# Block products in four groups, plain halves first, two fronts ahead, and raw x added when it is loaded for the fold

## The chip, the cores and the metric

The kernel runs on one core of a Trainium2 chip. The metric is the device time in microseconds (us) of one execution; lower is better. A profiled execution also has a span, from its first instruction to its last, and a granted TensorE clock (1.00 is full speed). TensorE is PE in the profile, VectorE DVE, ScalarE ACT, GpSimd POOL, and SP is the engine whose queue issues the transfers here.

## The reference

The input x has 2048 tokens of 448 channels. Cut to what is computed:

```
xn = layernorm(x)
A  = irfft2(rfft2(xn) * (w_r + i w_i))                  # spectral filter
h  = gelu(layernorm(xn) @ w1), four channel quarters shifted by +1, -1, +2, -2 tokens
x1 = xn + shifted(h) @ w2
B  = x1 + gelu(layernorm(x1) @ w3) @ w4                 # w3: 448 -> 1792, w4: 1792 -> 448
out = x + A + B
```

## The kernel before, in words

Each float32 operand of a large product is split into two float16 halves, and a product is three matmuls: high by high, high by low, low by high. The 2048 tokens are 16 blocks `b` (tokens a*16 + b); `xt` holds the running state of each block, read with `xb(b)`, in a scale that the factor `p12` undoes. The work runs in five stages: the first layer norm with w1 and w2 (to about 87 us); the MLP of group 0 (to about 112 us); the fold and first half of the transform beside the MLP of groups 1 and 2 (to about 190 us); the filter, 16 chunks, beside groups 2 to 4 (to about 275 us); the inverse transform, one block after another, beside groups 4 to 7.

**The MLP.** A group `G` (0 to 7) is two blocks, 256 tokens, and it is done in seven units `fp`, each of 256 of the 1792 hidden columns. `front(G, fp)` (L755) makes 22 matmuls of 256 columns into a PSUM bank `pw` (L433), applies the gelu on ACT (L763), and splits the result into the halves `hf`: high on ACT (L767), low on DVE (L768). `back(G, fp)` (L778) multiplies by w4. A plain unit makes 12 matmuls of 448 columns into `acc` (L798). A unit for which `crossed(G, fp)` holds (groups in `STR`) keeps only the 4 high-by-high matmuls of 448 columns. Its other two passes are block products with seven small products instead of eight (a Strassen form): three more DVE instructions make the combined operands `hg` (L771 to L773), 14 matmuls of 224 columns go to `acc` and to a second pair of banks `cr` (L809), and at the group's end ACT copies the banks `cr` to `cross` (L826) and POOL joins them (L829, L833; DVE does this for group 7). The combined weights come from `w4_forms` on POOL, once, for all groups. At a group's end `evacuate` (L815) adds `acc`, times a factor `k34`, to the state (L818).

`mlp(Gs, ahead)` (L837) sets the order in the program: `back` of a unit comes after the fronts of the next `ahead` units. Groups 0 to 2 have `ahead=AH=2`; later calls have 1. A scheduler then orders the instructions of each engine by priority, with `behind(...)` as a pin behind another instruction; matmuls of the MLP fill what the other stages leave. `hf` has three buffers, `hg` two, `pw` two banks.

**The fold.** `do_fold(b0)` (L568) loads raw x of two blocks into `xf` (three buffers; L571), normalizes it in place on ACT (L575), folds it on POOL (L580 to L583); `step1_in` splits it (ACT L591, DVE L592), `step1` multiplies (PE L601) and stores (ACT L605, DVE L606).

**The inverse.** `inv_a(b)` (PE `pe` L724, ACT L728, POOL L731 and L732, DVE L733 to L736, ACT L738, DVE L739) and `inv_b(b)` (PE `py` L746), which adds the filter's result to the state (DVE L747). For blocks 0 to 11 `finish(b)` (L560) then loads raw x into one of two row buffers `xr` (L556), adds `p12` times the state to it (DVE L557) and stores it (L561). Blocks 12 to 15, whose group is done last, have their raw x added into buffers in `x2mem` by the same L557 before the last `evacuate`.

Of the kernel before, what the change touches and what calls it, by code (L numbers as in the profile page):

```python
# [16 lines left out]
ALU = mybir.AluOpType  # L17
# [14 lines left out]
AH = 2  # L32
# [3 lines left out]
WMAX = [(1, 4), (1, 5), (2, 0), (2, 0), (2, 1), (2, 2), (2, 3), (2, 4)]  # L36
LATE = [(2, 2), (2, 3), (2, 4), (2, 5)]
HS = 3
STR = (5, 6, 7)
INV, LAG = 4, 2  # L40
EVAC, FILL = 0, 100000

# [80 lines left out]
def body(tc, nc, x, wf, w1, w2, w3, w4, c_g, c_n, c_small, out):  # L123
# [429 lines left out]
    def unscaled(b, t=None):  # L553
        if t is None:
            t = row()[:, :D]
        SY.dma_start(t, xv[:, b])  # L556
        V.scalar_tensor_tensor(out=t, in0=xb(b), scalar=p12, in1=t, op0=ALU.mult, op1=ALU.add)  # L557
        return t

    def finish(b):  # L560
        SY.dma_start(ov[:, b], unscaled(b))  # L561


    OFF = [0, 113, 225, 338, 450]
    FAM = [0, 2, 1, 3]
    folds = {}

    def do_fold(b0):  # L568
        f = pfd.tile([128, 2, 4, 113], F32, tag="xf", bufs=3, name=f"xf{b0}")
        X = f.rearrange("p b s d -> p (b s d)")[:, 0:2 * D + 2].rearrange("p (b d) -> p b d", b=2)  # L570
        after["X", b0] = (SY.dma_start(X[:, :, 0:D], xv[:, b0:b0 + 2]).ins,)  # L571
        with behind("f", *FOLD[b0 // 2]):
            for i in range(2):
                x_ = X[:, i, 0:D]
                A.activation(out=x_, in_=x_, func=AF.Identity, scale=xn_scale[b0 + i], bias=xn_bias[b0 + i])  # L575
            A.activation(out=X[:, :, D:D + 1], in_=X[:, :, 0:1], func=AF.Copy)
        ad = X[:, :, 0:D].rearrange("p b (h d) -> p h b d", h=2)[:, :, :, 0:113]
        bc = X[:, :, 1:D + 1].rearrange("p b (h d) -> p h b d", h=2)[:, ::-1, :, 223:110:-1]
        u = xr.rearrange("p (a b s d) -> p a b s d", a=2, b=2, s=2)
        P.tensor_tensor(out=u[:, 0], in0=ad, in1=bc, op=ALU.add)  # L580
        P.tensor_tensor(out=u[:, 1], in0=ad, in1=bc, op=ALU.subtract)
        for k, op in ((0, ALU.add), (2, ALU.subtract)):
            i = P.tensor_tensor(out=f[:, :, k:k + 2].rearrange("p b s d -> p s b d"), in0=u[:, :, 0], in1=u[:, :, 1], op=op)  # L583
        after["fold", b0] = (i.ins,)
        for i in range(2):
            folds[b0 + i] = f[:, i].rearrange("p s d -> p (s d)")
# [33 lines left out]
    def w_scale_end(wm):  # L620
        t = pc.tile([128, 4], F32, name="wt")
        V.tensor_reduce(out=t[:, 0:1], in_=wm, axis=AX.X, op=ALU.max)
        pt = bank("sp", "wpt")
        T.transpose(pt[0:1, 0:128], t[:, 0:1], ident)
        V.tensor_reduce(out=t[0:1, 1:2], in_=pt[0:1, 0:128], axis=AX.X, op=ALU.max)
        V.tensor_scalar(out=t[0:1, 1:2], in0=t[0:1, 1:2], scalar1=2.0 ** -20, scalar2=None, op0=ALU.max)
        pb = bank("sp", "wpb")
        T.matmul(pb[:, 0:1], ones[0:1], t[0:1, 1:2], start=True, stop=True)
        e = pc.tile([128, 3], I32, name="we")
        V.tensor_copy(out=t[:, 2:3], in_=pb[:, 0:1])  # L630
        V.tensor_single_scalar(e[:, 0:1], t.bitcast(I32)[:, 2:3], 0x7F800000, op=ALU.bitwise_and)
        V.tensor_single_scalar(e[:, 1:2], e[:, 0:1], 0x7F800000, op=ALU.bitwise_xor)
        V.tensor_scalar(out=sc[:, 0:1], in0=e.bitcast(F32)[:, 1:2], scalar1=ZPRE, scalar2=None, op0=ALU.mult)
        for h in range(2):
            V.tensor_scalar(out=sc[64 * h:64 * h + 64, 2:3], in0=sc[64 * h:64 * h + 64, 0:1], scalar1=2.0 * h - 1.0,
                            scalar2=None, op0=ALU.mult)
        V.tensor_scalar(out=sc[:, 1:2], in0=e.bitcast(F32)[:, 0:1], scalar1=2.0 ** -21 / (ZPRE * UPRE * VPRE),
                        scalar2=s12[:, 0:1], op0=ALU.mult, op1=ALU.mult)


    stream, pfs, zs = {}, {}, {}
# [100 lines left out]
    def inv_b(b):  # L742
        vh = vhs.pop(b)
        py = bank("sp", f"py{b}")
        for n, (vi, ri) in enumerate(PASS):
            T.matmul(py[:, :D], cV[ri], vh[:, vi], start=n == 0, stop=n == 2)  # L746
        V.scalar_tensor_tensor(out=xb(b), in0=py[:, :D], scalar=sc[:, 1:2], in1=xb(b), op0=ALU.mult, op1=ALU.add)  # L747


    acc, xs, hs, hg, rest = {}, {}, {}, {}, {}  # L750
# [27 lines left out]
    def back(G, fp):  # L778
        h = hs.pop((G, fp))
        n = D // 2  # L780
        end = 4 if G == 7 else 6
        if fp == 0:
            acc[G] = [bank("acc", f"acc{G}{i}") for i in range(2)]
            if G in STR:
                xs[G] = [bank("tr", f"cr{G}{i}") for i in range(2)]
        if (G, fp) == (7, 5):
            xs[G] = [bank("tr", f"end{i}") for i in range(2)]
        C = [[(slice(0, D), acc[G][i][:, 0:D], 0, 6)] for i in range(2)]
        if G == 7:
            C[1] = [(slice(0, D), acc[G][1][:, 0:D], 0, 4)]  # L790
            if fp > 4:
                C[1] = [(slice(n * k, n * k + n), xs[G][k][:, 0:n], 5, 6) for k in range(2)]
        for i in range(2):
            for r, to, s, e in C[i]:
                with behind("m", G, fp) if (G, fp) == (7, 6) and ("m", G, fp) in after else contextlib.nullcontext():
                    for f in range(2):
                        for hi, wi in ((0, 0),) if crossed(G, fp) else ((0, 0), (0, 1), (1, 0)):
                            m = T.matmul(to, h[:, hi, 2 * f + i], w4p[0][:, wi, 2 * fp + f, r],  # L798
                                         start=fp == s and f == 0 and hi + wi == 0, stop=fp == e and f == 1 and hi == 1)
                after["m", G, fp] = (m.ins,)  # L800
        if crossed(G, fp):
            g = hg.pop((G, fp))
            X = [xs[G][k // 2][:, n * (k % 2):n * (k % 2) + n] for k in range(4)]
            H = [[acc[G][i][:, n * k:n * k + n] for k in range(2)] for i in range(2)]
            forms = [(0, 1, X[0], 9), (1, 3, H[1][0], 9), (3, 2, H[0][0], C[0][0][3]), (6, 4, X[2], 9),
                     (4, 5, X[3], end), (5, 6, X[1], end), (2, 7, H[1][1], C[1][0][3])]
            for hi, wi in ((0, 1), (1, 0)):
                for k, slot, to, e in forms:
                    m = T.matmul(to, h[:, hi, slot] if slot < 4 else g[:, hi, slot - 4], w4f[fp][k][wi], start=k in (0, 6) and fp == 0 and hi == 0,  # L809
                                 stop=hi == 1 and fp == e)  # L810
            after["m", G, fp] = (m.ins,)
        k34 = p34[:, 1:2] if G >= 6 else p34[:, 0:1]
        to = {i: rest[2 * G + i] if G >= 6 else xb(2 * G + i) for i in range(2)} if fp >= 4 else {}

        def evacuate(i):  # L815
            for r, src, _, e in C[i]:
                if fp == e:
                    V.scalar_tensor_tensor(out=to[i][:, r], in0=src, scalar=k34, in1=to[i][:, r], op0=ALU.mult, op1=ALU.add)  # L818
                    if G == 7 and fp == 6:
                        SY.dma_start(ov[:, 2 * G + i, r], to[i][:, r])  # L820

        with prio(EVAC):
            if G in STR and fp == end:
                e0, e1 = cross[:, 0], cross[:, 1]
                for i in range(2):
                    A.activation(out=cross[:, i], in_=xs[G][i][:, 0:D], func=AF.Copy, scale=k34)  # L826
                for o, x, y in ((e0[:, n:], e0[:, 0:n], e0[:, n:]), (e1[:, 0:n], e1[:, 0:n], e0[:, n:]),
                                (e0[:, n:], e0[:, n:], e1[:, n:]), (e1[:, n:], e1[:, 0:n], e1[:, n:])):
                    (V if G == 7 else P).tensor_tensor(out=o, in0=x, in1=y, op=ALU.add)  # L829
            for i in range(2):  # L830
                evacuate(i)
                if G in STR and fp == end:
                    (V if G == 7 else P).tensor_tensor(out=to[i], in0=to[i], in1=cross[:, 1 - i], op=ALU.add)  # L833
                if G == 6 and fp == 6:
                    SY.dma_start(ov[:, 2 * G + i], to[i])
# [235 lines left out]
    xh_buf = [pfd.tile([128, 2 * 452 + 16], F16, name=f"xh{i}") for i in range(4)]  # L1071
    for i in range(4):
        P.memset(xh_buf[i][:, 904:], 0.0)
    mlp([1, 2], ahead=AH, tags=("mm", "tr"))
    for b in range(0, NB, 2):
        do_fold(b)
        step1_in(b)
        step1_in(b + 1)
        with behind("m", *PACE[b // 2]):
            step1(b)  # L1080
            step1(b + 1)
# [24 lines left out]
        if 0 <= i - 3 < NC:  # L1106
            chunk_c(i - 3)
    close("pst")
    mlp(range(3, 6))
    pv = pool("pv", side="right")  # L1110
    bs = [*range(12, 16), *range(8, 12), *range(8)]
    units = [(G, fp) for G in range(4, 8) for fp in range(7)][INV:]
# [11 lines left out]
                    finish(bs[n - 1])  # L1124

    inverse(range(4))
    mlp([6], last=True)
    inverse(range(4, 17))
    mlp([7], last=True)
    for name in ("pv", "pa2", "pa", "pw", "px", "pc", "ps"):  # L1130
# [25 lines left out]
```

## Time and profile before

| | |
|---|---|
| median of 3 runs | 410.98 us (409.61 to 411.87) |
| the profiled execution: time, span | 411.11 us, 409.2 us |
| granted clock | 1.00 |
| PE busy | 402.4 us, 98% of the span |
| DVE busy | 313.3 us, 77% |
| ACT busy | 268.2 us, 66% |
| POOL busy | 164.1 us, 40% |
| moved by DMA | 49.46 MB, mean 121 GB/s |

The busy time of PE is no measure of how well it is fed, since matmuls are pipelined: a record of 448 columns lasts 352 ns in the page's groups, though the next one starts 189 ns later (12 in 2.27 us in the chain). A wait of PE is therefore read from the starts: the time from one start to the next, less the step at which such matmuls follow each other undisturbed.

### The profile page before, as it was taken

The page shows a single profiled execution, that of the slowest core. Times are in us where ns is not written, and L with a number is a line of the kernel's source. Part 1 is how long each engine was busy: PE and PEld are TensorE (multiplying, and loading weights), DVE is VectorE, ACT ScalarE, POOL GpSimd, SP SyncE. Part 2 cuts the span into 40 slices and gives each one's busy share as a digit, 9 for nine tenths or more (in the row PEclk, how much of TensorE's full clock was granted, in tenths as well). Part 3 has the DMA queues.
Part 4 walks back from the last instruction along what each step waited for, and adds up shares of the span by engine and source line. Part 5 has one row for each costly group of instructions (what it writes and reads, how often), then busy time and mean ns, then how long its engine had stood idle before and what let it go on. Part 6 is the DMA issues. An engine that isn't in the chain of part 4 may idle for free.

```text
span 409.2 us, 8827 instructions
## 1 busy us (share of the span) xinstructions
PE 402.4 (98%) x3379; PEld 295.4 (72%) x3379; DVE 313.3 (77%) x674; ACT 268.2 (66%) x465; POOL 164.1 (40%) x260
## 2 busy tenths in 40 slices
PE   8999999999999999999999999999999999999996
PEld 3554555666677877677878887877788888878885
DVE  5989998898654737975899988841698969898645
ACT  4699993984838766754788888757566555644332
POOL 3889820002297745599321212100133234434300
PEclk9999999999999999999999999999999999999999
DMA  8999999907710356527367567320000202332201
GB/s 280 352 264 181 170 178 259 270 2 156 159 48 0 94 207 198 158 24 179 94 173 157 144 149 181 98 60 2 1 2 2 69 22 77 107 108 76 88 2 45
DMA packets 57209, 49.46 MB, mean 121 GB/s; under 512 B 41312, under 2 KB 52192, under 8 KB 57168
## 3 DMA queue, kind: packets, MB, share of 16 engines
q1 hardware_dynamic: 57168, 48.91, 46.3%
q8 instruction: 26, 0.43, 0.4%
q14 instruction: 15, 0.12, 0.1%
HBM read 35.06 MB, written 3.67 MB: 95 GB/s over the span
## 4 chain that ended last, share of the span: by engine, by line
PE 68%; DVE 12%; ACT 7%; DMA 6%; issue 3%; POOL 1%; SPq 0%; ACTq 0%; DVEq 0%; POOLq 0%
PE pw L433 23%; PE acc L798 18%; PE pw L462 6%; PE pw L507 6%; PE cr L809 3%; DMA wl<-wf 2%; PE acc L809 2%; ACT te L680 2%; PE ps L601 2%; PE py L746 2%; PE pe L724 2%; DVE te L683 1%; DVE te L681 1%; PE pu L704 1%; DMA h<-hs 1%
## 5 line engine op out<-in xcount | busy, mean ns | idle before, releaser
L433 PE MATMUL pw<-x2mem,w3p 128*128 128x256 f16 x1232 | 151.4, 272 | 0.0
L433 PEld LDWEIGHTS <-w3p 128*128 128x128 f16 x1232 | 118.8, 98 | 18.4
L798 PE MATMUL acc<-w4p,hf 128*128 128x448 f16 x508 | 106.7, 352 | 0.2 <-DVE xt L818 0.2
L798 PEld LDWEIGHTS <-hf 128*128 128x128 f16 x532 | 51.6, 98 | 37.1 <-issue 0.4
L768 DVE SCALAR_TENSOR_TENSOR hf<-pw,h,hf 128x512 f16<-128x512 f32 x56 | 41.8, 747 | 35.3 <-ACT hf L767 35.0
L763 ACT ACTIVATE pw<-pw,pe 128x512 f32<-128x512 f32 x56 | 36.7, 655 | 42.5 <-PE pw L433 42.4
L731 POOL TENSOR_TENSOR e<-e 128x226 f32<-128x226 f32 x16 | 12.8, 801 | 72.0 <-ACT e L728 67.9
L767 ACT ACTIVATE hf<-pw,h 128x512 f16<-128x512 f32 x56 | 38.3, 685 | 1.3
L507 PE MATMUL pw<-w2p,h 112*128 112x448 f16 x192 | 38.9, 352 | 0.1
L685 POOL TENSOR_TENSOR xr<-te 128x450 f32<-128x450 f32 x16 | 16.2, 1012 | 56.5 <-DVE te L683 50.6
L462 PE MATMUL pw<-w1p,w4x 128*128 128x448 f16 x176 | 34.9, 352 | 0.5 <-DVE h L936 0.5
L507 PEld LDWEIGHTS <-h 112*128 112x128 f16 x192 | 18.5, 98 | 16.8 <-DMA h<-x2mem 0.8
L462 PEld LDWEIGHTS <-w4x 128*128 128x128 f16 x176 | 17.0, 98 | 16.5 <-ACT w4x L422 0.7
L728 ACT ACTIVATE e<-pe 128x452 f32<-128x452 f32 x16 | 8.7, 544 | 20.7 <-PE pe L724 20.7
L580 POOL TENSOR_TENSOR xr<-xf 128x452 f32<-128x452 f32 x8 | 8.9, 1109 | 27.0 <-issue 16.0
L716 ACT ACTIVATE U<-y 113x512 f16<-113x512 f16 x32 | 18.0, 619 | 0.0
L592 DVE TENSOR_TENSOR xh<-xf,xh 128x452 f16<-128x452 f32 x16 | 14.0, 907 | 5.0 <-ACT xh L591 5.0
L680 ACT ACTIVATE te<-px 64x450 f32<-64x450 f32 x32 | 17.3, 539 | 0.6
L583 POOL TENSOR_TENSOR xf<-xr 128x452 f32<-128x452 f32 x16 | 16.7, 1066 | 0.6
L809 PE MATMUL cr<-w4x,hg 128*128 128x224 f16 x102 | 15.8, 259 | 0.1
L809 PEld LDWEIGHTS <-hg 128*128 128x128 f16 x152 | 14.7, 98 | 1.2 <-DVE hg L772 0.5
L738 ACT ACTIVATE vh<-e 128x448 f16<-128x448 f32 x16 | 9.2, 573 | 8.8 <-DVE e L736 8.8
(201 smaller groups left out, 773.1 us busy)
## 6 DMA issues: line engine op xcount, KB each, us to landing
wc<-wf SPq DMA_DIRECT2D x32, 225.0 KB, 3.7
wl<-wf SPq DMA_DIRECT2D x8, 450.0 KB, 3.7
xf<-x SPq DMA_DIRECT2D x8, 448.0 KB, 3.6
xt<-x SPq DMA_DIRECT2D x3, 896.0 KB, 11.0
w3raw<-w SPq DMA_DIRECT2D x3, 896.0 KB, 14.4
xr<-x SPq DMA_DIRECT2D x12, 224.0 KB, 2.6
out<-xr SPq DMA_DIRECT2D x12, 224.0 KB, 2.0
gn<-c_g SPq DMA_DIRECT2D x16, 128.0 KB, 3.3
```

The costliest lines, as they stand in the source:

```text
L433: T.matmul(ps_out, wp[:, wi + t, cols], xT[:, xi + t, tok], start=t == 0 and wi + xi == 0, stop=t == 3 and wi == 4)
L462: m = T.matmul(pm[:, :D], xTs[g][:, xi + t, 128 * i:128 * i + 128], w1p[:, wi + t], start=t == 0 and p == 0, stop=t == 3 and p == 2)
L507: m = T.matmul(w2b[b][:, :D], hT[g][:112, 4 * hi + k, o:o + 128], w2p[:, wi, k], start=k == 2 and hi + wi == 0, stop=k == 3 and hi == 1)
L583: i = P.tensor_tensor(out=f[:, :, k:k + 2].rearrange("p b s d -> p s b d"), in0=u[:, :, 0], in1=u[:, :, 1], op=op)
L680: i = A.activation(out=e[64 * h:64 * h + 64], in_=px_[64 - 64 * h:128 - 64 * h, :2 * DF], func=AF.Copy)
L685: P.tensor_tensor(out=z, in0=t[:, 0], in1=t[:, 1], op=ALU.add)
L716: A.activation(out=U[b][:113, p].rearrange("p q (c k) -> p q c k", c=NC), in_=Y1[:113, p, :, :, b], func=AF.Copy)
L763: A.activation(out=pm, in_=pm, func=AF.Gelu_apprx_tanh, scale=r3)
L767: i = A.activation(out=h[:, 0], in_=pv_, func=AF.Copy, scale=h3)
L768: j = V.scalar_tensor_tensor(out=h[:, 1], in0=pv_, scalar=h3, in1=h[:, 0], op0=ALU.mult, op1=ALU.subtract)
L798: m = T.matmul(to, h[:, hi, 2 * f + i], w4p[0][:, wi, 2 * fp + f, r], start=fp == s and f == 0 and hi + wi == 0, stop=fp == e and f == 1 a ...
L809: m = T.matmul(to, h[:, hi, slot] if slot < 4 else g[:, hi, slot - 4], w4f[fp][k][wi], start=k in (0, 6) and fp == 0 and hi == 0, stop=hi ...
```

## The change

Group 4 is computed by block products too. In the crossed units, all matmuls whose left operand is a plain half come before those with a combined operand. Groups 3 to 6 run with two fronts ahead. For the block pairs in `EARLY` (blocks 2 to 11) raw x is added to the state, times `p12`, when x has been loaded for the fold; `inv_b` then uses a factor that contains `p12`, the evacuations use the unscaled factor, and `finish` stores straight from the state. The first three fold loads are written ahead of the MLP of groups 1 and 2.

```diff
+EARLY = (2, 4, 6, 8, 10)
-STR = (5, 6, 7)
+STR = (4, 5, 6, 7)
...
     def finish(b):
-        SY.dma_start(ov[:, b], unscaled(b))
+        SY.dma_start(ov[:, b], xb(b) if b // 2 * 2 in EARLY else unscaled(b))
...
-    def do_fold(b0):
+    Xs = {}
+
+    def load_fold(b0, pin):
         f = pfd.tile([128, 2, 4, 113], F32, tag="xf", bufs=3, name=f"xf{b0}")
         X = f.rearrange("p b s d -> p (b s d)")[:, 0:2 * D + 2].rearrange("p (b d) -> p b d", b=2)
         after["X", b0] = (SY.dma_start(X[:, :, 0:D], xv[:, b0:b0 + 2]).ins,)
+        Xs[b0] = f, X
+        if b0 in EARLY:
+            with behind("f", *pin):
+                for i in range(2):
+                    V.scalar_tensor_tensor(out=xb(b0 + i), in0=xb(b0 + i), scalar=p12, in1=X[:, i, 0:D], op0=ALU.mult, op1=ALU.add)
+
+    def do_fold(b0):
+        f, X = Xs.pop(b0)
         with behind("f", *FOLD[b0 // 2]):
...
+        V.tensor_tensor(out=sc[:, 3:4], in0=sc[:, 1:2], in1=p12, op=ALU.mult)
...
-        V.scalar_tensor_tensor(out=xb(b), in0=py[:, :D], scalar=sc[:, 1:2], in1=xb(b), op0=ALU.mult, op1=ALU.add)
+        V.scalar_tensor_tensor(out=xb(b), in0=py[:, :D], scalar=sc[:, 3:4] if b // 2 * 2 in EARLY else sc[:, 1:2], in1=xb(b),
+                               op0=ALU.mult, op1=ALU.add)
...
-            for hi, wi in ((0, 1), (1, 0)):
-                for k, slot, to, e in forms:
+            for hi, wi, part in ((0, 1, 0), (1, 0, 0), (0, 1, 1), (1, 0, 1)):
+                for k, slot, to, e in forms[3 * part:3 + 4 * part]:
...
-        k34 = p34[:, 1:2] if G >= 6 else p34[:, 0:1]
+        k34 = p34[:, 1:2] if G else p34[:, 0:1]
...
+    for b in (0, 2, 4):
+        load_fold(b, (0, 6))
     mlp([1, 2], ahead=AH, tags=("mm", "tr"))
     for b in range(0, NB, 2):
+        if b > 4:
+            load_fold(b, FOLD[b // 2])
         do_fold(b)
...
-    mlp(range(3, 6))
+    mlp(range(3, 6), ahead=AH)
...
-    mlp([6], last=True)
+    mlp([6], last=True, ahead=AH)
```

## The prediction

> **What bounds the kernel now.** I read the page first, then the chain of waits in order of time, then the busy times by stage.
>
> ```profile
> PE 402.4 (98%) x3379; PEld 295.4 (72%) x3379; DVE 313.3 (77%) x674; ACT 268.2 (66%) x465; POOL 164.1 (40%) x260
> ```
>
> PE is busy throughout by its records, but records overlap the next matmul, so the share says neither how well PE is fed nor what a removed matmul is worth. The chain shows both. Its columns are start, length, what.
>
> ```profile
> 104.14 2.40 PE pw L433 x22
> 106.54 2.27 PE acc L798 x12
> 108.81 2.40 PE pw L433 x22
> ...
> 344.16 1.95 DMA out<-xr
> 346.12 2.92 DMA xr<-x
> ...
> 385.47 2.40 PE pw L433 x22
> 387.88 0.76 PE acc L798 x4
> 389.97 2.40 PE pw L433 x22
> ```
>
> A front follows a back without a gap in nearly all of the run: PE is the bound, by the work that it is given, and each matmul costs its step (2.40/22 = 0.109 us for 256 columns, 2.27/12 = 0.189 for 448). A plain unit takes 108.81 - 104.14 = 4.67 us, a crossed one 389.97 - 385.47 = 4.50, of which the 14 small matmuls are 389.97 - 387.88 - 0.76 = 1.33 (0.095 each). Only around 335 to 362 us does the chain leave PE for DVE and for the row buffer that is stored and loaded again (1.95 and 2.92 us at 344 to 349). Busy times by stage (length, then PE, PEld, DVE, ACT, POOL, then clock, DMA share and GB/s):
>
> ```profile
> 112.50:145.00 32.50, 32.50 (x281) 24.18 (x279) 17.78 (x23) 20.82 (x39) 27.69 (x30) 1.00 0.20 58
> ...
> 190.00:250.00 60.00, 59.54 (x629) 48.10 (x626) 52.28 (x92) 48.18 (x88) 18.00 (x21) 1.00 0.64 158
> 250.00:270.00 20.00, 20.00 (x197) 15.93 (x195) 15.23 (x25) 14.05 (x25) 3.92 (x4) 1.00 0.39 102
> 270.00:285.00 15.00, 15.00 (x128) 11.00 (x126) 4.77 (x7) 9.92 (x19) 0.00 (x0) 1.00 0.09 26
> 285.00:330.00 45.00, 45.00 (x426) 36.69 (x424) 35.38 (x82) 26.71 (x48) 11.57 (x16) 1.00 0.07 22
> 330.00:362.00 32.00, 31.73 (x302) 26.02 (x300) 27.17 (x61) 17.63 (x32) 13.62 (x18) 1.00 0.23 73
> 362.00:385.00 23.00, 23.00 (x210) 19.08 (x209) 20.58 (x43) 10.45 (x17) 10.03 (x12) 1.00 0.30 101
> ```
>
> DVE is the second engine: 52.3 of 60 us in the filter, 83.1 of 100 us in the inverse stage (285 to 385). What PE loses to it is read from the starts, in the timeline of PE:
>
> ```profile
> 242.73 0.42 PE L658 MATMUL pp<-csm,y 113*128 113x112 f16 x5
> 243.42 0.74 PE L675 MATMUL px<-x2mem,gn 128*128 128x225 f16 x6 [0.28 <-DVE te L681]
> ...
> 341.91 0.82 PE L433 MATMUL pw<-x2mem,w3p 128*128 128x256 f16 x6
> 342.93 0.73 PE L746 MATMUL py<-vh,csm 128*128 128x448 f16 x3 [0.20 <-DVE xt L747]
> ...
> 357.83 0.60 PE L433 MATMUL pw<-x2mem,w3p 128*128 128x256 f16 x4
> 358.49 0.27 PE L809 MATMUL cr<-w4x,hg 128*128 128x224 f16 x1
> ```
>
> Six matmuls from 341.91 take 6 x 0.109 = 0.65, so `py` could have started at 342.56 and lost 0.36; the four from 357.83 lost 0.22; at 243.42 about 0.44 went. Reading all matmul rows of the stages so (281 from 112.5, 629 from 190, 302 from 330, and so on), PE loses 0.04 us from 112.5 to 145, 0.54 to 170, 0.05 to 190, 1.81 in the filter to 250, 0.10 to 285, and 0.23 + 0.99 + 0.16 = 1.38 in the inverse: 3.9 us together. That bounds what better feeding can give. The 7.5 us that PE loses before 112.5 lie ahead of everything that changes.
>
> **Part by part.** The profiled execution took 411.11 us with a span of 409.2, 1.9 us outside; it stands 0.13 us above the median of the runs, 410.98. I sum against 411.11. About 0.5% (2.05 us) is what a measurement can tell from no change.
>
> *Products.* Seven units of group 4 go from plain to crossed: 7 x (4.67 - 4.50) = **-1.2 us**. PE is the bound there (270 to 285: 15.00 of 15.00 busy, 0.10 lost in 250 to 285), so this counts in full. Plain halves first and two fronts ahead change no matmul.
>
> *The new operands.* Each of the seven units adds the three DVE instructions of `hg`, and group 4 adds two ACT copies and six POOL additions at its end.
>
> ```profile
> L771 DVE TENSOR_TENSOR hg<-hf 128x512 f16<-128x512 f16 x19 | 8.3, 435 | 0.4
> L773 DVE TENSOR_TENSOR hg<-hf,hg 128x256 f16<-128x256 f16 x19 | 8.2, 433 | 0.3
> L772 DVE TENSOR_TENSOR hg<-hf,hg 128x256 f16<-128x256 f16 x19 | 8.0, 419 | 0.3
> ...
> 335.01 2.86 POOL L829 TENSOR_TENSOR x2mem<-x2mem 128x224 f32<-128x224 f32 x4 [3.01 <-ACT x2mem L826]
> ...
> 337.45 0.70 DVE L771 TENSOR_TENSOR hg<-hf 128x512 f16<-128x512 f16 x1
> 338.19 1.11 DVE L772 TENSOR_TENSOR hg<-hf,hg 128x256 f16<-128x256 f16 x1
> 339.33 1.10 DVE L773 TENSOR_TENSOR hg<-hf,hg 128x256 f16<-128x256 f16 x1
> ```
>
> At the mean a unit adds 0.435 + 0.433 + 0.419 = 1.29 us of DVE, 9.0 for seven. From 250 to 285 DVE is busy 15.23 + 4.77 = 20.0 of 35 us, so they fit on the whole; from 250 to 270, where four units fall beside the filter's last chunks, 4.77 us are idle and 5.2 are wanted. The excess of 0.4 is covered by the second front: in the changed instruction order, PE does a back of one unit and a front of 2.40 us between a unit's front and its back that were not there between them before. I take 0; without that cover it is +0.4, at the price beside a running POOL (0.70 + 1.11 + 1.10 = 2.9) it is the second rival. POOL's additions (2.86 us for four of the six) fall after group 4, where POOL is busy 11.57 of 45 us.
>
> *The row buffers.* Ten loads, ten L557 and ten store-and-reload chains leave the inverse.
>
> ```profile
> L557 DVE SCALAR_TENSOR_TENSOR xr<-xt,s,xr 128x448 f32<-128x448 f32 x12 | 10.3, 862 | 1.5 <-DMA xr<-x 1.4
> L557 DVE SCALAR_TENSOR_TENSOR xr<-xt,s,xr x12: 670/686/1557, 319.2 to 379.1; 128x448 f32<-128x448 f32 x12
> ```
>
> That is 10 x 0.862 = 8.6 us of DVE out of 83.1, and the waits at 344 to 349 go, since the store then reads the state. DVE falls to about 75 of 100 us. With two fronts ahead, the chain from gelu to `hg` also gets a front more of time. PE's 1.38 us of losses are of these two kinds (`py` behind a late L747, `cr` behind a late `hg`); I take 1.1 of it: **-1.1 us**, between 0 and -1.38. What is late next is PE itself.
>
> *The filter.* Groups 3 and 4 run here with two fronts ahead. The losses at `px` (0.44 at 243.42) come from the filter's own chain on DVE, which no front shortens, but more MLP work is ready to be put before a late `px`. Bounds 0 and -1.81; I take **-0.4**, nearer to nothing, as the chain is untouched.
>
> *The early additions.* Ten DVE additions move into 112 to 150. Four of them stand right behind the last `hf` of group 0, ahead of the split (L592) for the first fold product.
>
> ```profile
> 112.66 0.75 DVE L768 SCALAR_TENSOR_TENSOR hf<-pw,h,hf 128x512 f16<-128x512 f32 x1 [3.79 <-ACT hf L767]
> 114.44 1.79 DVE L592 TENSOR_TENSOR xh<-xf,xh 128x452 f16<-128x452 f32 x2 [1.02 <-ACT xh L591]
> ...
> L899 POOL TENSOR_TENSOR w4x<-w4p x12: 596/608/997, 114.7 to 181.6; 128x224 f16<-128x224 f16 x12
> ...
> 118.29 1.50 PE L601 MATMUL ps<-csm,xh 128*128 128x128 f16 x24
> ```
>
> At 0.69 to 1.56 each (median and longest of L557) they end between 116.2 and 119.6, and L592 between 118.0 and 121.4; in the changed order PE wants the low halves after two passes of each block and four front matmuls, at 118.29 + 4 x 0.06 + 4 x 0.109 = 119.0. The loss lies between 0 and 2.5 us. The nearest row is L592 itself, two SBUF operands in the same place beside the same POOL work, 0.90 each: four of these end at 117.0, L592 at 118.8, and I take **+0.2**.
>
> The Trainium skill, "SBUF — State Buffer", section "Who interferes with whom", goes further: a DVE instruction with two SBUF inputs and a GpSimd one that reads SBUF share an exclusive lock, and the later one waits for all of the other. By that rule each of the four additions would wait for a whole POOL instruction, and the sum would end at the first rival's time. By that rule, the trace agrees as far as it goes: the longest L557 takes 1.56 us against a median of 0.69, and the longest L899 1.00 against 0.61.
>
> The other six additions follow `hf` of group 1, and the ACT normalization of the same pair waits for them, with the split L591 of the pair before and the next gelu behind it. That is about 1.7 us for two additions; the product `ps` of blocks 4 and 5, the tightest, has more room:
>
> ```profile
> 134.78 2.51 DVE L592 TENSOR_TENSOR xh<-xf,xh 128x452 f16<-128x452 f32 x2 [1.34 <-ACT xh L591]
> 139.90 1.50 PE L601 MATMUL ps<-csm,xh 128*128 128x128 f16 x24
> ```
>
> L592 ends at 137.29, 2.6 us ahead of PE: nothing lost. On SP, three row loads (L556) move ahead of the last fold load and of the eight `wl` loads:
>
> ```profile
> 149.32 1.40 SPq L556 DMA_DIRECT2D x2mem<-x  x3
> 155.58 14.54 SPq L615 DMA_DIRECT2D wl<-wf  x6
> ```
>
> DVE waits for `wl`, with `hf` and the evacuation of group 1 behind it, and PE loses 0.54 at 164. Between -0.54 and +1.4 (the three issues) I take 0, since the same bytes are ahead of the third `wl` load either way.
>
> Sum: -1.2 - 1.1 - 0.4 + 0.2 = -2.5, so 411.11 - 2.5 = **408.6 us**; its own range is 407.6 to 409.6.
>
> **Rivals.** *First, the early additions meet POOL.* Each of the four waits for a whole POOL instruction; at 0.69 + 0.61 = 1.30 us they end at 118.6, L592 at 120.4, and PE loses 1.0 to 1.4 at the first fold product instead of 0.2: 409.4 to 409.8. For it: POOL is busy 27.69 of 32.5 us. Against it: PE can put front work between.
>
> *Second, slower.* In 250 to 270 the `hg` instructions run at the price beside POOL, 2.9 a unit: four units want 11.7 us, 6.9 more than are idle. Less the front of 2.40 that the second front lends, PE waits 4.5 us: 411.11 - 1.2 - 1.1 + 0.2 + 4.5 = 413.5. It decides from (4.77 + 2.40)/4 = 1.8 us a unit on. Against it: POOL is busy only 3.92 of these 20 us.
>
> *Third, the second front also takes away most of the filter's losses*, 1.4 instead of 0.4: 407.6, and 406.7 with all of the inverse's 1.38 and the 0.54 around 164. For it: PE has a front more to do while `px` is late. Against it: in the row at 243.42 PE stood although front matmuls followed right behind; their order is fixed before the run.
>
> That the change doesn't do what it says can be excluded: in the changed instruction order group 4 has 14 small matmuls a unit, and `back(5, 0)` stands behind `front(5, 2)`.
>
> **How the numbers follow.** Forecast 0.45, first rival 0.20, second 0.15, third 0.20. The line for faster is 410.98 - 2.05 = 408.93: it takes in about two thirds of the forecast's own range and all of the third rival, 0.30 + 0.20 = 0.50. Slower is the second rival, 0.15; the rest, 0.35, is within 0.5%. The range goes from 406.6, the third rival's low end, to 411.6: 408.6 with 2.3 more at the first fold product and 0.7, half of the bound, at the `wl` loads; the second rival is left out.
>
> **What would show it.** A crossed unit of group 4 with 4.50 us from front to front when nothing else lies between; no loss at `py` and `cr` from 285 to 385, and DVE near 75 of 100 us there; `ps` of blocks 0 and 1 on PE no later than 119.2; DVE idle again by 275. Wrong it would be if PE's starts show a new gap of over 1 us at 118 or from 250 to 285, or if the inverse keeps its gaps with DVE less busy.

## The result: 412.6 us, half a per cent slower, where 408.6 was forecast

The changed kernel takes 412.61 us (median of 16 executions, 410.31 to 414.90), the kernel before beside it 410.75 (409.61 to 411.87): a ratio of 1.0047, interval 1.0032 to 1.0062. A second set gave 413.04 against 410.87, ratio 1.0045 (1.0029 to 1.0062). The profiled execution of the changed kernel took 411.86 us with a span of 409.3, about as before (411.11 and 409.2), and with its mean clock at 1.00; so two things have to be found: what took the expected 2.5 us in that execution, and what makes others longer still.

The page of the changed kernel, busy time of each engine (line numbers of the changed kernel are 1 higher up to the fold and 11 to 13 higher behind it: `hf` is L781, the evacuation of a group L831, `px` L687):

```profile
PE 400.4 (98%) x3421; PEld 299.7 (73%) x3421; DVE 324.5 (79%) x696; ACT 269.1 (66%) x467; POOL 167.6 (41%) x266
```

PE has 2.0 us less and DVE 11.2 us more to do. Busy times by stage (same columns as in the prediction):

```profile
112.50:145.00 32.50, 32.37 (x279) 24.03 (x278) 23.28 (x29) 19.62 (x37) 25.92 (x27) 1.00 0.15 44
145.00:170.00 25.00, 22.98 (x199) 17.28 (x198) 18.29 (x25) 16.83 (x31) 13.63 (x13) 1.00 0.61 194
...
250.00:270.00 20.00, 19.65 (x195) 16.15 (x193) 18.49 (x35) 15.29 (x28) 3.93 (x4) 1.00 0.43 114
270.00:285.00 15.00, 15.00 (x151) 12.93 (x149) 9.48 (x20) 10.34 (x18) 0.98 (x1) 1.00 0.14 40
285.00:330.00 45.00, 45.00 (x444) 38.36 (x442) 36.09 (x81) 27.24 (x49) 15.61 (x22) 1.00 0.03 11
330.00:362.00 32.00, 32.00 (x315) 27.08 (x314) 25.98 (x61) 18.87 (x34) 12.21 (x16) 1.00 0.10 38
362.00:385.00 23.00, 23.00 (x210) 19.08 (x209) 16.38 (x37) 9.60 (x16) 9.04 (x12) 1.00 0.18 71
```

In the inverse (the last three rows) PE is full, as forecast. The new hole is in the second row: PE has 22.98 of 25 us. The same row of the kernel before:

```profile
145.00:170.00 25.00, 24.78 (x224) 18.77 (x223) 16.80 (x24) 16.89 (x31) 10.86 (x11) 1.00 0.59 186
```

The timeline of PE around the hole, first the kernel before, then the changed one:

```profile
162.06 2.56 PE L433 MATMUL pw<-x2mem,w3p 128*128 128x256 f16 x22
164.84 1.29 PE L798 MATMUL acc<-w4p,hf 128*128 128x448 f16 x6 [0.22 <-DVE xt L818]
```

```profile
161.85 2.56 PE L434 MATMUL pw<-x2mem,w3p 128*128 128x256 f16 x22
166.44 1.29 PE L811 MATMUL acc<-w4p,hf 128*128 128x448 f16 x6 [2.02 <-DVE xt L831]
```

The back of group 2's first unit needs the PSUM bank that DVE's evacuation of group 1 frees. It comes 1.6 us later, and by the starts PE loses 2.18 us here instead of 0.38. What DVE did ahead of that evacuation, in its timeline of before and of after:

```profile
154.47 1.09 DVE L268 TENSOR_REDUCE wm<-wl 128x1 f32<-128x900 f32 x1 [2.24 <-DMA wl<-wf]
...
159.62 1.09 DVE L268 TENSOR_REDUCE wm<-wl 128x1 f32<-128x900 f32 x1 [1.81 <-DMA wl<-wf]
...
164.12 0.67 DVE L818 SCALAR_TENSOR_TENSOR xt<-acc,p,xt 128x448 f32<-128x448 f32 x1
```

```profile
157.16 2.18 DVE L269 TENSOR_REDUCE wm<-wl 128x1 f32<-128x900 f32 x2 [2.83 <-DMA wl<-wf]
159.25 0.74 DVE L781 SCALAR_TENSOR_TENSOR hf<-pw,h,hf 128x512 f16<-128x512 f32 x1
161.43 1.09 DVE L269 TENSOR_REDUCE wm<-wl 128x1 f32<-128x900 f32 x1 [1.44 <-DMA wl<-wf]
...
165.71 0.68 DVE L831 SCALAR_TENSOR_TENSOR xt<-acc,p,xt 128x448 f32<-128x448 f32 x1
```

DVE waits 2.83 and 1.44 us for `wl`, with the evacuation queued behind. It waited as long before (2.24 and 1.81 us), but its first reduction of `wl` stood 2.69 us earlier. The loads are late because SP issued them late, in SP's timeline of before and of after:

```profile
147.92 0.37 SPq L571 DMA_DIRECT2D xf<-x  x1
148.38 0.89 SPq L615 DMA_DIRECT2D wl<-wf  x2
```

```profile
147.34 1.84 SPq L557 DMA_DIRECT2D x2mem<-x  x4
150.48 0.38 SPq L574 DMA_DIRECT2D xf<-x  x1
150.91 0.94 SPq L626 DMA_DIRECT2D wl<-wf  x2
```

The last fold load waits for a buffer of the fold, and `wl` is queued behind it: both come 2.5 us later, and four row loads instead of one are ahead of them. Why the buffer comes late is told by the additions' own view (duration min/median/max, first and last start; then who waited for them), and by ACT's timeline in both kernels:

```profile
L579 DVE SCALAR_TENSOR_TENSOR xt<-xt,s,xf x10: 672/919/1454, 112.8 to 152.2; 128x448 f32<-128x448 f32 x10
...
  ACT xf L586: 5.0, 4
```

```profile
132.55 1.41 ACT L575 ACTIVATE xf<-xf,nm,vw 128x448 f32<-128x448 f32 x2
...
145.61 1.05 ACT L591 ACTIVATE xh<-xf 128x452 f16<-128x452 f32 x2 [0.93 <-POOL xf L583]
```

```profile
134.44 0.76 ACT L586 ACTIVATE xf<-xf,nm,vw 128x448 f32<-128x448 f32 x1 [1.99 <-DVE xt L579]
...
140.58 0.76 ACT L586 ACTIVATE xf<-xf,nm,vw 128x448 f32<-128x448 f32 x1 [1.47 <-DVE xt L579]
...
148.63 1.05 ACT L602 ACTIVATE xh<-xf 128x452 f16<-128x452 f32 x2 [2.70 <-POOL xf L594]
```

The normalization in place may not overwrite raw x before DVE has added it; DVE adds only behind `hf`; so ACT stood 5.0 us in four waits, three of them (4.0 us) ahead of the split of blocks 8 and 9. POOL folded later, and that split, which frees the buffer for the last fold load, came at 148.63 instead of 145.61. The prediction had looked at `ps` of blocks 4 and 5 alone, and that product was in time.

### The profile page after: what moved, and what is told of

Read it like the earlier page. It is cut to its first block, busy times and chain, and to the rows that moved or that the text cites. A ratio compares the mean times of both kernels' runs of the same rounds, so it can differ in the third digit from the quotient of the medians.

```text
span 409.3 us, 8929 instructions
## 1 busy us (share of the span) xinstructions
PE 400.4 (98%) x3421; PEld 299.7 (73%) x3421; DVE 324.5 (79%) x696; ACT 269.1 (66%) x467; POOL 167.6 (41%) x266
## 4 chain that ended last, share of the span: by engine, by line
PE 42%; ACT 9%; DVE 6%; DMA 2%; issue 2%; POOL 1%; SPq 0%; DVEq 0%; POOLq 0%; ACTq 0%
PE pw L434 17%; PE acc L811 9%; PE cr L822 5%; PE acc L822 4%; ACT te L692 3%; PE pe L736 2%; DMA wl<-wf 2%; PE py L758 2%; ACT zb L704 2%; DVE te L695 1%; ACT y L719 1%; ACT x2mem L677 1%; DVE te L693 1%; PE ps L612 1%; POOL xr L697 1%
## 5 line engine op out<-in xcount | busy, mean ns | idle before, releaser
L434 PE MATMUL pw<-x2mem,w3p 128*128 128x256 f16 x1232 | 149.4, 273 | 0.0
L811 PE MATMUL acc<-w4p,hf 128*128 128x448 f16 x452 | 96.3, 352 | 2.0 <-DVE xt L831 2.0
L811 PEld LDWEIGHTS <-hf 128*128 128x128 f16 x476 | 46.1, 98 | 33.3 <-issue 2.2
L781 DVE SCALAR_TENSOR_TENSOR hf<-pw,h,hf 128x512 f16<-128x512 f32 x56 | 41.8, 746 | 32.4 <-ACT hf L780 32.2
L743 POOL TENSOR_TENSOR e<-e 128x226 f32<-128x226 f32 x16 | 10.8, 677 | 65.2 <-ACT e L740 55.9
L822 PEld LDWEIGHTS <-hg 128*128 128x128 f16 x208 | 20.0, 98 | 0.1
L822 PE MATMUL cr<-w4x,hg 128*128 128x224 f16 x138 | 19.3, 259 | 0.0
L822 PEld LDWEIGHTS <-hf 128*128 128x128 f16 x156 | 15.0, 98 | 4.6
L603 DVE TENSOR_TENSOR xh<-xf,xh 128x452 f16<-128x452 f32 x16 | 15.3, 996 | 3.3 <-ACT xh L602 3.3
```

The costliest lines, as they stand in the source:

```text
L434: T.matmul(ps_out, wp[:, wi + t, cols], xT[:, xi + t, tok], start=t == 0 and wi + xi == 0, stop=t == 3 and wi == 4)
L603: j = V.tensor_tensor(out=t[:, 452:904], in0=f, in1=t[:, 0:452], op=ALU.subtract)
L781: j = V.scalar_tensor_tensor(out=h[:, 1], in0=pv_, scalar=h3, in1=h[:, 0], op0=ALU.mult, op1=ALU.subtract)
```

## The experiments

The theories. **T1**: the early additions make the fold, its last load and with it `wl` late; DVE waits for `wl` in front of the evacuation; PE waits at 164. **T2**: the row loads now ahead of `wl` on SP do it. **T3**: the time goes elsewhere (`hg` in group 4, the second front). **T4** and **T5** came up later, for the longer executions: T4, a fetch of instructions among the last stores; T5, the granted clock falling behind a long stall.

**Which part costs.** Edits to the changed kernel, and (third) to the kernel before:

```
e2_no_early      EARLY = ()              # all raw x added in the inverse again
e14_early_six    EARLY = (6, 8, 10)      # the six additions at 133 to 153 us alone
e10_early_two    EARLY = (2, 4)          # the four additions at 113 us alone
e3_early_only    before + EARLY = (2, 4, 6, 8, 10); STR = (5, 6, 7), one front ahead, old pass order
e7_one_front     EARLY = (), mlp(range(3, 6)) and mlp([6], last=True) without ahead=AH
```

> The changed kernel without the early additions: the list of early blocks is empty, so all blocks load their rows and add in the inverse as before; the crossed products of group 4, the plain halves first and the two fronts ahead stay. T1 and T2 expect the loss at 164 us to go back to about 0.4 us and the time to 410 to 411 us (the products' gain of 1.2 us stays, part of the inverse's 1.1 us is lost). T3 expects 412 or more, as in the changed kernel.

> The kernel before with the early additions alone: raw x added to ten blocks' state at the fold, and nothing else of the change. T1 and T2 expect it slower than before by 1 to 2.5 us (2 us at 164 us, less up to 1 us gained in the inverse): 411.5 to 413.5. T3 expects it no slower than before: 409.5 to 411.

> The changed kernel with early additions for two pairs only, blocks 2 to 5: their four additions at 113 us stay, the six in the middle of group 1 go back to the inverse. T1 expects the fold and the last fold load at their times of before, the loss at 164 us under 0.6, 0.3 to 0.4 at the first fold product, part of the inverse's gain kept: 410 to 410.7. If the four additions at 113 us are what costs, 412 or more.

> The changed kernel with early additions for blocks 6 to 11 only: the six additions in the middle of group 1 stay, the four at 113 us go back to the inverse. T1 expects the last fold load and the wl loads as late as in the changed kernel, a loss of about 2 us at 164 us, none at the first fold product, and 412 to 413. If it takes all ten to make the fold late, 410.5 or less.

> The changed kernel without the early additions and with one front ahead instead of two in groups 3 to 6: what stays is the crossed products of group 4 and the plain halves first. T3 (the second front in the filter costs) expects PE's losses from 190 to 285 us to fall from 2.6 to 1.9 us or less, the losses in the inverse stage to return to about 1.4 us, and 410.3 to 411 us in all, about as without the early additions (410.7). If the second front costs nothing there, the losses from 190 to 285 stay at 2.6 and the time is 411 to 411.5.

| kernel | us, median (range) | before beside it | ratio (interval) | PE's loss 145 to 170 |
|---|---|---|---|---|
| changed kernel, two sets | 412.61, 413.04 | 410.75, 410.87 | 1.0047, 1.0045 | 2.23, 2.28 |
| no early additions | 410.70 (409.36-413.85) | 410.81 | 0.9995 (0.9977-1.0013) | 0.21 |
| early additions alone | 413.85 (413.33-416.21) | 410.81 | 1.0083 (1.0059-1.0106) | 2.47 |
| the four at 113 us | 410.03 (409.18-411.40) | 411.05 | 0.9979 (0.9967-0.9992) | 0.21 |
| the six in group 1 | 411.90 (410.75-414.55) | 410.68 | 1.0032 (1.0014-1.0049) | 4.08 |
| no early, one front | 411.36 (410.07-412.22) | 410.87 | 1.0005 (0.9989-1.0021) | 0.61 |

T1 holds and T3 falls as the main cause: the early additions alone make the kernel before 3.0 us slower, and without the six in the middle of group 1 the loss at 164 is gone. Two sizes were missed: the early additions alone were expected at 411.5 to 413.5, and the six at a loss of about 2 us, where 4.08 was measured (the clock, below, is in it). With the four alone, SP's, DVE's and PE's timelines show it:

```profile
147.79 0.37 SPq L574 DMA_DIRECT2D xf<-x  x1
148.25 0.89 SPq L626 DMA_DIRECT2D wl<-wf  x2
```

```profile
152.95 1.09 DVE L269 TENSOR_REDUCE wm<-wl 128x1 f32<-128x900 f32 x1 [0.85 <-DMA wl<-wf]
```

```profile
161.93 2.57 PE L434 MATMUL pw<-x2mem,w3p 128*128 128x256 f16 x22
164.38 1.29 PE L811 MATMUL acc<-w4p,hf 128*128 128x448 f16 x6
```

The fold load and `wl` are issued at their times of before, and PE loses 0.21 us. This version is 1.0 us under the kernel before, and the shortest of those in the table. The run with one front was to show whether the second front costs something in the filter: PE's losses from 190 to 285 were 2.48 us with one front and 2.61 with two, so in sum it does not, though the losses lie at other places (see the part on the prediction). Without it PE lost 2.65 us in the inverse instead of 1.51 (both without early additions). So of the two cases put for it the second came (411 to 411.5), though the inverse lost more than the 1.4 us expected.

**Where on the way to wl.**

```
e1_wl_early   with behind("X", 14): -> with behind("X", 12):       # around wm = w_scale()
e9_rows_late  three of the four row loads issued behind the first two wl loads
e4_wm_late    WMAX = [(2,0),(2,0),(2,1),(2,1),(2,2),(2,2),(2,3),(2,4)]
e11_two_wm    e10_early_two with the WMAX of e4_wm_late
```

> The changed kernel, with the step that loads and reduces the wl tiles allowed two fold pairs earlier: on SP two of the first wl loads then stand ahead of the three row loads and the third ahead of the last fold load, and DVE's first reductions of wl stand earlier. T1 (the early additions delay the fold, the last fold load and with it the wl loads, and DVE waits for wl in front of the evacuation of group 1) expects the loss of PE at 164 us to fall from 2.2 us to under 0.6, and 410 to 411 us against 412.6 of the changed kernel. T2 (the row loads ahead of the wl loads cost it) expects the same, since the order is turned round too. T3 (the time is lost elsewhere: hg in group 4, two fronts ahead in the filter) expects no change: 412 or more.

> The changed kernel with three of the four row loads held back until the first two wl loads are issued: SP's order is then that of the kernel before, with all early additions kept. T2 (the row loads' bytes, 0.69 MB, ahead of the first wl load delay it) expects the first reduction of wl about 2 us earlier (155.2 us instead of 157.2), the loss at 164 us under 0.6, and 410.5 to 411.2. T1 (the additions delay the fold loads, and with them wl, whatever stands between) expects the loss at 164 us to stay over 1.5, and 412 or more.

> The changed kernel with the list of places for the reductions of wl moved behind: only two of them are left ahead of the evacuation of group 1 on DVE, and hf of the first unit of group 2 goes before them; the order of the loads on SP stays. T1 expects most of the loss at 164 us to go, as the evacuation no longer waits behind a late wl: 410 to 411 us. T2, if it is the lateness of the loads itself that costs (whoever needs wl later waits for it), expects the loss to move to a later place and the time to stay at 412 or more. T3 expects no change.

> As the run before, and with the places for the reductions of wl moved behind as in the run with the late reductions, so that a late wl can't hold back the evacuation of group 1. Expected from the two effects together: no loss at 164 us, 409.5 to 410.5, and fewer executions over 411 than the run before; nothing over it, if wl is in time anyway.

Measured: 412.13 us for the first (ratio 1.0030, 1.0017 to 1.0044; loss from 145 to 170 of 1.21), 411.05 for the second (1.0013, 0.9991 to 1.0035; 1.02), 411.33 for the third (1.0005, 0.9987 to 1.0022; 0.03), 410.28 for the fourth (0.9976, 0.9964 to 0.9989; 0.03). The first brought less than T1 expected: the third wl load, which waits for a buffer, now stood ahead of the last fold load and held it back to 153.35 us, and the split of that pair stood late in front of the evacuation; PE also lost 0.9 us more in the filter than in the changed kernel. The second has all additions and SP's order of before. Its SP and DVE timelines:

```profile
151.43 0.37 SPq L575 DMA_DIRECT2D xf<-x  x1
151.89 0.89 SPq L627 DMA_DIRECT2D wl<-wf  x2
```

```profile
156.77 2.24 DVE L269 TENSOR_REDUCE wm<-wl 128x1 f32<-128x900 f32 x2 [1.50 <-DMA wl<-wf]
```

From the last fold load's issue to the first reduction it is 5.34 us; in the changed kernel 157.16 - 150.48 = 6.68. That would give the row loads some 1.3 us of the lateness. But the kernel before, with SP's order of this run, takes 154.47 - 147.92 = 6.55 there, and the version with four additions, in the same order, 152.95 - 147.79 = 5.16: the stretch differs by 1.4 us between kernels with one order, and what moves it stays open. Against the kernel before the first reduction is 2.69 us late, and 2.56 us of that are the late issue, which the additions cause. So T2 is not shown to have a share in the lateness, though this run, 1.6 us shorter than the changed kernel's first set, leaves it possible; its loss and its first reduction lie between what T1 and T2 expected. The third confirms the last link: with only two reductions ahead of the evacuation the loss at 164 went, though the loads were no earlier (152.57 against 150.91, in an execution that ran 1.7 us late by then); 0.72 us came back further on, where a later wait for `wl` (1.07 us, DVE at 172.07) held up a fold product:

```profile
175.79 1.50 PE L612 MATMUL ps<-csm,xh 128*128 128x128 f16 x24 [0.56 <-DVE y L617]
```

The fourth has the shortest execution on record (408.58), but its median isn't under that of the four additions alone: where `wl` is in time, its places don't matter.

**Why some executions are 2 us longer.** Of the changed kernel's 28 executions 11 have a mean granted clock of 0.993 to 0.996, and their median is 414.0 (eight of the first set's 16) and 413.5 (three of the second set's 12); the other 17 have 411.7 and 412.9. So the clock separates the long executions in the first set; in the second, five took 412.85 to 413.75 at 0.999 or more, and what made those long stays open. Of the 104 executions of before that stand beside the experiments one has such a clock.

```
e0_after_again   no edit
e5_pad_after     each of the 22 first warm-up matmuls of 512 columns cut into three: 44 more matmuls
e6_pad_before    the kernel before with 42 more warm-up matmuls, made in the same way
e8_wl_twice      for _ in range(2 if c == 0 else 1): the first wl load issued twice
e13_wl_nine      range(9 if c == 0 else 1): issued nine times
```

> The changed kernel again, unedited, beside the next three. T1 (late wl loads) alone expects a span of about 409.6 us in every execution and a time of 411.7. T4 (a last fetch of 16 KB of PE instructions, which the program before doesn't have, falls among the packets of the final stores in some executions: in the trace of the kernel without early additions it started at 406.1 us and the final two stores took 3.6 us instead of 1.8) expects part of the executions longer by about 2 us, with a mean granted clock under 0.997, since PE idles longer at the end: median 412 to 413.

> The changed kernel with its 22 first warm-up matmuls cut into three pieces each: 44 more matmuls and 44 more weight loads on PE in the first 8 us, where PE waits for data, and no other work. The last fetch of PE instructions then comes some 88 instructions, about 4.4 us, earlier. T4 expects it to be over before the final stores: no execution with a clock under 0.997, and a median 0.5 to 1 us under the unedited kernel's of the same runs (411.7 or so). T1 alone expects no difference between the two.

> The kernel before with its warm-up matmuls cut into pieces, so that PE has as many instructions as in the changed kernel (42 more matmuls and weight loads in the first 8 us), and nothing else changed. T4 expects a 27th fetch of 16 KB near the end, and part of the executions longer by about 2 us with a clock under 0.997: median 411 to 412 against 410.8 of before. T1 and T3 expect 410.8 as before.

> The changed kernel with the first wl load issued twice, so that all wl data come later by the time of a 450 KB load or more. T1 expects the loss of PE at 164 us to grow from 2.2 us to 4 us or more and the time to grow at least by as much. T5 (where this stall lasts long enough, the granted TensorE clock falls to a half behind it for one step of its record, 3.4 us, and PE loses half of that, 1.7 us; this is what makes half of the changed kernel's executions 2 us longer than the others, at a mean granted clock of 0.996) expects a clock row of 0.5 right behind 164 us in the trace, a mean clock of 0.996 in every execution, and about 1.7 us beside the stall: 416 us or more. Without T5 the clock stays at 1.0 there and the time is 414 to 416.

> The changed kernel with the first wl load issued nine times, so that wl comes 8 us later or so (a second copy had cost 1.05 us at the first reduction). T1 expects a loss of PE at 164 us of 4 to 7 us. T5 (a stall of PE of that length lets the granted TensorE clock fall to a half behind it, for one step of its record, 3.4 us, so that PE loses 1.7 us more) expects a clock row of 0.5 behind 164 us in the trace, a mean clock of 0.996 or less, and matmuls of 256 columns at twice their step there. Without T5 the clock stays at 1.0 behind the stall, and the executions at 0.996 have another cause.

T4 came from the run without early additions, whose DMA view gives for the last two stores a landing of

```profile
out<-x2mem SPq DMA_DIRECT2D x2, 112.0 KB, 3.6
```

against 1.8 us before. As the cause of the low clock it falls: with the matmuls added to the changed kernel, 416.01 us (1.0123, 1.0099 to 1.0148), the last fetch started at 400.45, clear of the stores, and five of six executions still had 0.991 to 0.996. The kernel before with as many instructions (414.55; 1.0094, 1.0074 to 1.0114) settles nothing here: none of its four executions is under 1.0, but its last fetch, at 406.14, was over before the last stores, which were issued from 407.78 on. That both are 3 us slower is a result of its own: cutting warm-up matmuls is not free. Part of it stands at 164 us again (losses of 3.46 and 1.49 from 145 to 170) and some 0.75 us at 38 us, where PE waits for a transfer (`h`); why they come, and the rest, stays open.

T5 is seen in two traces. The profiled execution with the six additions was one of the long ones. Its PE timeline and its stages (clock is the third number from the end):

```profile
160.99 2.57 PE L434 MATMUL pw<-x2mem,w3p 128*128 128x256 f16 x22
165.78 1.62 PE L811 MATMUL acc<-w4p,hf 128*128 128x448 f16 x6 [2.22 <-DVE xt L831]
167.19 2.97 PE L434 MATMUL pw<-x2mem,w3p 128*128 128x256 f16 x13
```

```profile
164.00:167.00 3.00, 1.23 (x6) 0.63 (x6) 3.00 (x6) 2.97 (x7) 0.00 (x0) 0.93 0.70 229
167.00:170.00 3.00, 3.00 (x16) 1.94 (x14) 3.00 (x5) 0.54 (x1) 2.86 (x3) 0.50 0.50 143
```

PE stands 2.2 us, and behind it 13 matmuls take 2.97 us, 0.228 each, where 22 had taken 2.57, 0.117 each: the clock is at a half from 166.6 to 170.0. Half of 3.4 us, 1.7, is lost beside the stall's 2.38; together the 4.08 of the table. A mean clock of 0.996 is what one such step makes of it: 0.5 x 3.4 / 410 = 0.004 less than 1. Smaller falls can have another place: the profiled execution without early additions has 0.997, and its clock fell at 407.8, behind PE's last matmul, while the late stores ran. With nine wl loads (420.15 us; 1.0223, 1.0201 to 1.0244) PE stands longest at 184 and 195, not at 164 as expected, since only two reductions were left ahead of the evacuation there; the clock falls behind both stalls, here behind the first:

```profile
184.00:188.00 4.00, 0.30 (x2) 0.05 (x1) 1.45 (x2) 0.53 (x1) 4.00 (x8) 1.00 0.67 168
188.00:191.00 3.00, 2.71 (x25) 2.66 (x25) 2.49 (x4) 2.90 (x6) 2.38 (x5) 0.52 0.52 154
```

The run with two wl loads decided nothing (412.05 us; 1.0033, 1.0016 to 1.0051): the first reduction came 1.05 us later, but the loss at 164 hardly grew (2.39), as DVE's later waits for `wl` shrank.

The traces also show why only some executions are hit. The clock record changes on a grid of 3.41 us (406.2 us at full clock are 119 such steps). In the run with the six additions the 2.38 us without a matmul lay in one step of the grid, and the clock fell; with nine loads 3.41 and 2.61 lay in one step, and it fell twice; in the changed kernel's profiled execution 2.2 us were split 1.09 and 1.10 over two steps, in the second set 1.30 and 0.95, with 44 more matmuls 1.59 and 1.85 (3.43 together, more than the 2.38), and it stayed. That the place of the stall on the grid differs from one execution of a kernel to the next is inferred: each kernel has one trace, the changed one two. That the changed kernel's own 11 executions are of this kind is inferred from their mean clock; no trace of one of them was taken.

The Trainium skill, "TensorE: Matmul & The Clock Gate", section "HAM oscillation — how this bites in real kernels", asks for no idle gaps of PE over about 3.4 us. Here a gap of 2.4 us was enough when it fell into one step.

The Trainium skill, "TensorE: Matmul & The Clock Gate", section "What's actually happening", gives a free-running window of 3413 ns. The grid of 3.41 us seen here agrees with it.

## Why the prediction was wrong, step by step

- **Products**, -1.2: right. The chain of the changed kernel has a crossed unit of group 4 (a front and a back) in 279.01 to 283.51, 4.50 us:

```profile
279.01 2.40 PE pw L434 x22
...
283.51 0.76 PE acc L811 x4
```

- **Inverse**, -1.1: right in kind and nearly in size. PE's losses from 285 to 385 went from 1.38 to 0.26 + 0.18 + 0.09 = 0.53, a gain of 0.85, with none at `py` or `cr`. DVE fell from 83.1 to 36.09 + 25.98 + 16.38 = 78.5 of 100 us, not to 75.
- **Filter**, -0.4: wrong in sign. Losses went from 1.81 to 2.02 in 190 to 250, and from 0.10 to 0.65 in 250 to 285, most of it 0.52 us at a late `px`, +0.8 in all. The versions with one front lose 0.70 to 0.78 from 250 to 285 too, but at another place: 0.60 of it where PE waits for the gelu on ACT, and nothing at that `px`. First the changed kernel, then the run with one front and no early additions:

```profile
266.21 0.74 PE L687 MATMUL px<-x2mem,gn 128*128 128x225 f16 x6 [0.35 <-DVE te L693]
```

```profile
281.75 0.93 PE L811 MATMUL acc<-w4p,hf 128*128 128x448 f16 x4 [0.44 <-ACT hf L780]
```

So the second front, which was to make a late `px` cheaper, goes with the late `px`: the traces of all versions with two fronts but one (that with nine `wl` loads, late by other waits) have it, early additions or not. In the changed kernel DVE works without a pause from 261.57 until the `te` at 265.38 that `px` waits for, and two `hg` instructions of 0.43 and 0.28 us are in that stretch. That is the second rival's mechanism at an eighth of its price; that the `hg` make the difference was not tested alone.
- **Early additions at the first fold product**, +0.2: right, 0.30 to 0.38 by the starts of PE. The four took 4.09 us, 1.02 each, where 0.90 was taken and the first rival had 1.30; the measurement lies between. The first rival's price is what the rule of the Trainium skill, "SBUF — State Buffer", section "Who interferes with whom", would give for additions that each wait for a whole POOL instruction; the trace shows less.
- **The other six additions**, "nothing lost": the step that failed. It saw ACT's normalization wait, and followed that wait to `ps` alone. The same wait also holds the fold's buffers, so the last fold load (2.56 us later), so everything queued behind it on SP, `wl` above all.
- **The wl loads**, 0 between -0.54 and +1.4: mis-sized by the same step. The argument that the same bytes are ahead of the third `wl` load either way left out the time at which SP can issue it: 158.28 us instead of 155.58. Measured: 2.23 - 0.54 = +1.7, over the upper bound, which had priced three issues on SP and not a late buffer.
- **Not in the sum at all**: the half clock behind the stall, 1.7 us where it comes, by the mean clock in 11 executions of 28.

In the profiled execution: -1.2 - 0.85 + 0.76 + 0.33 + 1.7 = +0.7, where -2.5 was forecast. Of these 3.2 us the `wl` loads make 1.7 and the filter 1.2. PE lost some 0.4 us less ahead of 112.5 than before, which nothing in the change accounts for, and its last matmul began at 405.69 in both. The long executions lift the median from there, in the first set those with the low clock; in the second set that accounts for little of it.

The signs that the prediction had named for being wrong were gaps at 118, from 250 to 285 and in the inverse; none of them looked at 164, although the sum has its bound of +1.4 there. The rivals: the first (additions meet POOL) had the place right that didn't matter; the second was right that it could be slower, but the time was lost mainly by another mechanism; the third is refuted. By the third rival's own terms its low end is 406.8, not 406.7 or 406.6, which changes nothing here.

## What to carry to other kernels

When a step makes an in-place operation wait, follow the wait to the buffer that it holds, from there to the load that wants the buffer, and along that load's queue; the first consumer being in time proves nothing about the others. On a kernel bound by PE, don't queue a reduction that waits for a DMA ahead of the instruction that frees a PSUM bank. And a stall's price isn't only its length: one of 2.4 us that fell within one step of the clock's grid cost half a step, 1.7 us, more, so look at the mean clock of every execution, not only at the one that was profiled.

## What the runs showed of the hardware that was not expected

- The granted clock fell to a half for 3.4 us after only 2.38 us without a matmul within one 3.41 us step of its grid; 1.85 us in one step left it at 1.00.
- Cutting the 22 warm-up matmuls of the first 8 us into two or three pieces each, with the same columns in all, made the two kernels 3.0 and 3.7 us slower.
- An instruction fetch of 16 KB among the last stores went with a landing of 3.6 us instead of 1.8, in one execution; that the fetch is the cause is not shown.
